# Layer 0 of an interleaved attention kernel: memory part added once per segment, two-chunk maps, filler matmuls

## Chip, cores, metric

One core of one Trainium2 chip. The metric is device time of one launch in microseconds (us), the span of the core. Ratios are the mean time of one kernel's fast runs over that of the other's of the same rounds, so not quite the ratio of the medians that I quote; brackets are 95% intervals.

## The reference, cut

Four layers over 2048 tokens of 512 features, 32 heads of 16: layers 0 and 2 are "A", layers 1 and 3 "B".

```python
def _A_ref(x, wq, wk, wv, wo, beta):             # 4 segments of 512 tokens
    ...
    for s in range(N):
        p = _softmax(qs @ ks * scale + mask)      # local attention, causal
        a_dot = p @ vs
        a_mem = (phi(qs) @ M) / (phi(qs) @ z + 1e-6)   # memory of earlier segments
        o = g * a_mem + (1.0 - g) * a_dot
        M = M + phi(ks).T @ vs ; z = z + sum(phi(ks))
    return concat(o) @ wo
def _B_ref(x, wqkv, wo): ...                      # full attention, 2048 x 2048
x = x + A(ln(x)); x = x + B(ln(x)); x = x + A(ln(x)); x = x + B(ln(x))
```

phi(t) is t+1 for positive t, else exp(t). So a segment of an A layer has a local part (softmax attention) and a memory part, which needs everything that earlier segments put into M and z.

## The kernel before: the parts concerned

The kernel is a program builder. It walks through the work with its own clock of each engine, decides at each moment what goes next, and emits fixed instruction streams. Attention units go first. Background threads (layer norm, projections, memory chain, output projection) get the PE when attention doesn't want it. ScalarE does the exponentials in groups of up to three 512-column tiles. Some quadruples of four tiles ("dz", "dx") get their exponential on VectorE instead. A table changes the builder's parameters every 110 groups, and strings give the order of A and B units:

```python
PAT = ["AAAAAAAA", "ABABABABBBABAAABBA", ...]
TUNE = [
    (0, {'CF': 0.829, 'PB': 0.02, 'DX_AHEAD': 0.5, 'DX_SLACK': 4.776, 'DX_LEAD': 69, ...}),
    (110, {'CF': 0.849, 'RATE': 0.472, 'MMC': 0.229}),
    ...                      # CF, PB, MMC, PV0: what the builder believes matmuls cost
```

`ensure(x)` makes the builder run background threads until x exists, and nothing else: each time the step that can start first, with 0.4 us added per place down the list of priorities. The end of a layer-0 chunk:

```python
if self.cnt[key] == 2:
    if A and s >= 2:
        self.ensure(("op", L, s - 2))        # buffer o0[s % 2] still feeds the projection of s-2
    ...
        o = dv(lambda e: e.transpose(dst, onf), ..., "oT", 0.73)
        if s > 0:
            self.ensure(("nd", L, s))        # memory part of this segment
            o = dv(lambda e: e.tensor_tensor(dst, dst, mem, ALU.add), ..., "oM", 0.43)
    self.chunk_done(L, s, c, zs, o)
```

and the test in front of a chunk's last value matmuls:

```python
if last and u["kind"] == "A" and u["s"] > 0 and (u["L"] > 0 or u["pvd"] == 4) and ("nd", u["L"], u["s"]) not in self.ev:
    return None
```

The memory part itself: eight steps of two products, reciprocal and multiply, then four transposing DMAs.

```python
for i in range(4):
    for hf in range(2):
        ...  # 2 matmuls ph x Mr ; den, reciprocal, multiply on DVE -> ot[i]
if L == 0:
    yield ("ev", [("pvdone", L, s - 1)])
    for i in range(4):
        self.dma_T(self.m0[:, :, i * 128:(i + 1) * 128], self.ot[:, i, :], ...)
self.set_ev(("nd", L, s), sc.t["dve"])
```

The maps phi work on chunks of 512 columns (exp on ACT; min, then max-and-add on DVE), 24 chunks of q and 24 of k. Filler matmuls exist (`keep_warm`), but are off (KEEP = 0).

The softmax here doesn't subtract the row's maximum and nothing guards it: scores larger than these inputs give would overflow.

## Time and profile before

| | before |
|---|---|
| median | 2082.59 us (2079.41 to 2085.5, 3 runs) |
| span of the profiled run | 2082.3 us |
| ACT busy / idle | 1990.4 / 91.9 us |
| mean granted TensorE clock | 0.649 |
| quadruples on VectorE | 109 |

A row of the profile's groups has line, engine, operation, output<-input, count, busy time and mean ns of one, then idle time before it and what ended it. In a timeline row a bracket is the engine's idle time just before, with its releaser. ACT is busy 96% of the time, so time is read from ACT's gaps and from what occupies it. The prediction shows the lines.

### The profile page before, as it was taken

What the parts mean: (1) busy time and instruction counts of PE and PEld (TensorE: products, weight loads), DVE (VectorE), ACT (ScalarE), POOL (GpSimd) and SP (SyncE); (2) the same over time, 40 slices, a digit from 0 to 9 for tenths busy, and PEclk for the clock granted to TensorE, in tenths of its full rate; (3) what the DMA queues carried; (4) which work ended last, traced back from release to release, by engine and by line L of the source; (5) the groups of instructions that cost most, each with busy time, mean ns of one, the idle gap of its engine ahead of it and who ended that gap; (6) DMA issues with size and microseconds to landing.
All of it is one profiled execution on the core that took longest, in us unless ns stands there. A gap on an engine that the chain in (4) does not pass through costs nothing.

```text
span 2082.3 us, 41423 instructions
## 1 busy us (share of the span) xinstructions
PE 1705.9 (82%) x17296; PEld 592.2 (28%) x17382; DVE 1645.9 (79%) x2492; ACT 1990.4 (96%) x1615; POOL 253.3 (12%) x564
## 2 busy tenths in 40 slices
PE   6768888888878888788787788888888888888887
PEld 2222221112311121212222223213444444444443
DVE  6886758887678688787878577688789988898986
ACT  6879899999999999999999999999999999999997
POOL 4542410001400000211013103100000000000000
PEclk9679897557565675557776797675655555555555
DMA  4210100001000000001010100100000000000000
GB/s 122 51 32 11 28 15 1 1 1 21 7 16 1 11 11 1 1 1 21 1 21 1 21 11 2 21 1 2 14 5 4 4 14 4 5 4 15 6 4 12
DMA packets 75467, 27.31 MB, mean 13 GB/s; under 512 B 68112, under 2 KB 74768, under 8 KB 75280
## 3 DMA queue, kind: packets, MB, share of 16 engines
q1 hardware_dynamic: 74176, 23.62, 5.2%
q8 instruction: 136, 2.23, 0.5%
q10 hardware_dynamic: 1104, 1.05, 0.2%
q14 instruction: 51, 0.42, 0.1%
HBM read 6.30 MB, written 2.10 MB: 4 GB/s over the span
## 4 chain that ended last, share of the span: by engine, by line
ACT 49%; PE 29%; issue 11%; DVE 7%; POOL 2%; DMA 1%; SPq 0%; ACTq 0%; DVEq 0%; POOLq 0%
ACT pT L1135 48%; PE ps L1128 13%; PE ps L625 6%; PE ps L1379 5%; PE ps L1397 4%; POOL pT L1158 2%; PE ps L1267 1%; DMA xT<-xn 1%; DVE lnst L662 1%; DVE T L1517 0%; DVE tokk L786 0%; ACT ph L780 0%; DVE ot L919 0%; SPq L444 0%; DVE db L1325 0%
## 5 line engine op out<-in xcount | busy, mean ns | idle before, releaser
L1135 ACT ACTIVATE pT<-ps 128x1536 bf16<-128x1536 f32 (+2 forms) x1525 | 1957.3, 1458 | 66.1 <-PE ps L1128 57.4
L1128 PE MATMUL ps<-q,kB 32*128 32x512 bf16 x3660 | 699.6, 546 | 256.3 <-ACT pT L1135 248.3
L1270 DVE TENSOR_SCALAR dz<-ps 128x512 int32<-128x512 f32 x436 | 301.0, 691 | 156.8 <-PE ps L1267 143.6
L1128 PEld LDWEIGHTS ps<-q,kB 32*128 32x128 bf16 x3660 | 131.4, 97 | 701.5 <-ACT pT L1135 656.1
L1158 POOL TENSOR_SCALAR_AFFINE_SELECT pT<-pT 128x256 bf16<-128x256 bf16 (+2 forms) x516 | 223.8, 463 | 613.4 <-ACT pT L1135 611.9
L1397 PE MATMUL ps<-pT,vB 128*17 128x512 bf16 x2216 | 278.7, 507 | 0.7 <-DVE q L640 0.5
L1267 PE MATMUL ps<-q,kB 32*128 32x512 bf16 x436 | 250.0, 573 | 0.0
L1379 PEld LDWEIGHTS ps<-vB,pT 128*128 128x128 bf16 x5776 | 181.1, 104 | 160.8 <-issue 157.6
L1379 PE MATMUL ps<-vB,pT 128*128 128x17 bf16 x5776 | 213.4, 177 | 0.7 <-ACT pT L1135 0.4
L1128 PE MATMUL ps<-q,kA 32*128 32x512 bf16 (+3 forms) x1024 | 122.4, 385 | 47.7 <-ACT pT L1135 45.6
L1307 DVE TENSOR_SCALAR df<-dz 128x2048 f16<-128x2048 uint16 x109 | 134.0, 1229 | 2.4
L1397 PEld LDWEIGHTS ps<-pT,vB 128*17 128x17 bf16 x2216 | 51.0, 89 | 187.0 <-issue 176.5
L1314 DVE TENSOR_SCALAR db<-dz 128x2048 int16<-128x2048 int16 x80 | 97.8, 1222 | 1.6 <-PE ps L1397 1.6
L1517 DVE STREAM_TRANSPOSE T<-ps 128x512 f32<-128x512 f32 x94 | 66.6, 709 | 15.3 <-PE ps L1397 14.7
L625 PE MATMUL ps<-xT,wB 128*128 128x512 bf16 x228 | 70.4, 429 | 7.4 <-issue 3.9
L625 PE MATMUL ps<-xT,wA 128*128 128x512 bf16 x238 | 68.7, 412 | 8.1 <-issue 2.1
L991 DVE TENSOR_TENSOR x_tok<-x_tok,ps 128x512 bf16<-128x512 bf16 x60 | 41.0, 686 | 41.6 <-PE ps L625 41.3
L1319 DVE TENSOR_TENSOR tokk<-tokk,df 128x2048 f16<-128x2048 f16 x58 | 70.7, 1219 | 0.7
L1323 DVE TENSOR_TENSOR tokk<-tokk,df 128x2048 f16<-128x2048 f16 x58 | 70.7, 1218 | 0.6
L1128 PEld LDWEIGHTS ps<-q,kA 32*128 32x128 bf16 x1024 | 29.9, 99 | 125.7 <-ACT pT L1135 110.9
L680 DVE TENSOR_SCALAR xn<-x_tok,lnmv,lnr 128x512 bf16<-128x512 bf16 x60 | 24.5, 429 | 50.3 <-DMA xT<-xn 49.4
L1325 DVE TENSOR_TENSOR db<-db,dz 128x2048 int16<-128x2048 int16 x51 | 62.8, 1231 | 1.2
(128 smaller groups left out, 1513.2 us busy)
## 6 DMA issues: line engine op xcount, KB each, us to landing
x_tok<-in_A_x_dram SPq DMA_DIRECT2D x14, 128.0 KB, 2.7
wB<-in_B_wqkv_dram SPq DMA_DIRECT2D x4, 384.0 KB, 3.9
out_dram<-x_tok SPq DMA_DIRECT2D x3, 512.0 KB, 3.0
xT<-xn SPq DMA_TRANSPOSE x60, 2.4
wA<-in_A_wk_dram SPq DMA_DIRECT2D x1, 512.0 KB, 7.7
wA<-in_A_wq_dram ACTq DMA_DIRECT2D x1, 512.0 KB, 7.9
wA<-in_A_wv_dram SPq DMA_DIRECT2D x1, 512.0 KB, 8.8
woA<-in_A_wo_dram SPq DMA_DIRECT2D x1, 512.0 KB, 7.5
```

The costliest lines, as they stand in the source:

```text
L625: return self.sc.add("pe", lambda e: e.matmul(out, lhsT, rhs, start=start, stop=stop), reads=reads, bank_ops=[(bank, "w", alloc)], emit=la ...
L1128: sc.add("pe", (lambda out, lhsT, rhs: lambda e: e.matmul(out, lhsT, rhs, start=True, stop=True))(out, lhsT, rhs), reads=reads, bank_ops=[ ...
L1135: o = sc.add("act", lambda e: e.activation(dst, src, ACT.Exp, scale=float(SCALE)), writes=[self.b_pT[s0 + i] for i in range(n)], bank_ops= ...
L1158: om = sc.add("pool", (lambda ap, pat: lambda e: e.affine_select(ap, ap, pattern=pat, compare_op=ALU.is_ge, fill=0.0, base=0, channel_mult ...
L1267: sc.add("pe", lambda e: e.matmul(out, lhsT, rhs, start=True, stop=True), reads=reads, bank_ops=[(bank, "w", alloc)], emit=True, name="SX" ...
L1270: o = sc.add("dve", lambda e: e.tensor_scalar(dst, out, float(EXP_C * 65536.0), -126.0 * 65536.0, op0=ALU.mult, op1=ALU.max), writes=[self ...
L1307: o = dv(lambda e: e.tensor_scalar(F, lo, 2.0 ** -16, -0.5, op0=ALU.mult, op1=ALU.add), bz, bF, "dF", 1.24)
L1314: o = dv(lambda e: e.tensor_scalar(E, hi, 128.0, 16256.0 + 53.0, op0=ALU.mult, op1=ALU.add), bz, bE, "dE", 1.24)
L1319: o = dv(lambda e: e.tensor_tensor(Pz, Pz, F, ALU.mult), bF + bP, bP, "dP2", 1.24)
L1323: o = dv(lambda e: e.tensor_tensor(Pz, Pz, F, ALU.mult), bF + bP, bP, "dP4", 1.24)
L1379: op = sc.add("pe", (lambda o0, w, v, first: lambda e: e.matmul(self.ps[:, o0:o0 + 17], w, v, start=first, stop=True, skip_group_check=Tru ...
L1397: sc.add("pe", (lambda out, v, rhs, start, stop: lambda e: e.matmul(out, v, rhs, start=start, stop=stop, skip_group_check=True))(out, v, r ...
```

## The change

Intent: the memory part should no longer hold up each chunk of layer 0. It is added to a whole segment later, by a background thread. Two chunks go through phi at once. And where PE would idle, matmuls with zero weights are meant to keep its clock high. Table and unit order were tuned anew. The core of the diff, cut:

```diff
-PAT = ["AAAAAAAA", "ABABABABBBABAAABBA", "BAAABBBAAAAA", "AAAAABABABAB", "AAAABABABBAA", "BBABAABAAA"]
+PAT = ["AAAAAAAA", "ABABABABBAABAABBBA", "AAAAABABBBAA", "AAAAABBABBAA", "AAAAABBBBAAA", "BBABAABAAA"]
-    (110, {'CF': 0.849, 'RATE': 0.472, 'MMC': 0.229}),
+    (110, {'DVE_AHEAD': 4.069, 'KEEP': 8.79}),
 ...                                             # all other rows too
+        if HALF and L % 2 == 0 and s > 0:       # q: mask, phi, mask on two chunks
+            cs = slice(2 * h, 2 * h + 2)
+            ...
+            yield from self.g_phi(L, s, qo, bo, self.ph[:, cs, :], self.b_ph[cs], f"q{c}", wide=True)
-            for c in range(NCH):                # k: phi on two chunks
+            for h in range(2):
 ...
             if self.cnt[k3] == 4:
+                self.set_ev(("pvl", L, s))
+                if L == 0 and s > 0:
+                    self.t_addmem(s, zs)
+                    return
+    def t_addmem(self, s, zs):
+            yield ("ev", [("nd", 0, s)])
+            ...
+            o = sc.add("dve", lambda e: e.tensor_tensor(dst, dst, mem, ALU.add), ..., name="oM", cost=1.24)
+            self.t_out(0, s, zs, self.prio_of(1, s) - 0.5, o.t_end)
-                if s > 0:
-                    self.ensure(("nd", L, s))
-                    o = dv(... "oM", 0.43)
-  ... and (u["L"] > 0 or u["pvd"] == 4) and ("nd", ...
+  ... and u["L"] > 0 and ("nd", ...
-            if KEEP and self.acc_open and t + d <= tc + KEEP_D and ... and self.pvu[0]["L"] <= KEEP_L:
+            if KEEP and t + d <= tc + KEEP_D and (...) <= sc.lately() < KEEP and self.keep_warm():
```

More of the change, by code (lines that the diff above doesn't have):

```diff
@@ L54 @@
 DX3 = 1
+HALF = True
 TUNE = [
-    (0, {'CF': 0.829, 'PB': 0.02, 'DX_AHEAD': 0.5, 'DX_SLACK': 4.776, 'DX_LEAD': 69, 'DVE_AHEAD': 4.525, 'MAXPV': 3, 'RATE': 0.606, 'MMC': 0.22, 'LN_G': 3, 'PV0': 0.371, 'DX3': 1}),
-    (110, {'CF': 0.849, 'RATE': 0.472, 'MMC': 0.229}),
-    (220, {'MMC': 0.213, 'PV0': 0.365}),
-    (330, {'LN_G': 2}),
-    (440, {'DVE_AHEAD': 2.5}),
-    (660, {'PB': 0.022}),
-    (880, {'PB': 0.026, 'RATE': 0.4}),
-    (990, {'MMC': 0.2, 'PV0': 0.324}),
-    (1100, {'CF': 1, 'PB': 0.025, 'DX_AHEAD': 0.676, 'LN_G': 3}),
-    (1210, {'PB': 0.036, 'DX_LEAD': 64, 'DVE_AHEAD': 3.61}),
-    (1320, {'DX_SLACK': 5.687}),
-    (1430, {'PB': 0.035, 'DX_LEAD': 53, 'DVE_AHEAD': 3.961, 'MAXPV': 2}),
+    (0, {'CF': 0.684, 'PB': 0.026, 'DX_AHEAD': 0.696, 'DX_SLACK': 4.776, 'DX_LEAD': 67, 'DVE_AHEAD': 4.525, 'MAXPV': 3, 'RATE': 0.606, 'MMC': 0.22, 'LN_G': 1, 'PV0': 0.371, 'DX3': 1, 'KEEP': 0.0, 'KEEP0': 3.0, 'KEEP_D': 0.0}),
+    (110, {'DVE_AHEAD': 4.069, 'KEEP': 8.79}),
+    (220, {'KEEP0': 4.5}),
+    (550, {'DX_SLACK': 6.455}),
+    (660, {'CF': 1}),
+    (770, {'MMC': 0.219, 'KEEP_D': 0.029}),
+    (880, {'PB': 0.037, 'DX3': 0}),
+    (990, {'DX_AHEAD': 0.893, 'MMC': 0.227, 'PV0': 0.34}),
+    (1100, {'PB': 0.038}),
+    (1210, {'MMC': 0.247}),
+    (1320, {'DX_SLACK': 8}),
+    (1430, {'CF': 0.748}),
 ]
@@ L320, in alloc @@
         self.ph = sb("ph", [P, NCH, 512], bf)
-        self.et = sb("et", [P, 512], bf)
+        self.et = sb("et", [P, 1024], bf)
         self.tokk = sb("tokk", [P, 4, D], bf)
@@ L346, in alloc @@
         self.gm = sb("gm", [P, NCH, 136], bf)
-        self.bmf = sb("bmf", [P, 136], f32)
+        self.bmf = self.et[:, 0:272].bitcast(f32)
         self.parm = sb("parm", [P, 2], f32)
@@ L397, in alloc @@
         self.b_gm = B("gm")
-        self.b_bmf = B("bmf")
+        self.b_bmf = self.b_et
         self.b_parm = B("parm")
@@ L769, in g_q @@
             return
+        if HALF and L % 2 == 0 and s > 0:
+            h = c // 2
+            key = ("cnt_q", L, s, h)
+            self.cnt[key] = self.cnt.get(key, 0) + 1
+            if self.cnt[key] < 2:
+                return
+            cs = slice(2 * h, 2 * h + 2)
+            qo, qe = self.q[:, z, 1, cs, :], self.q[:, z, 0, cs, :]
+            bo, be = self.b_q[z][1][cs], self.b_q[z][0][cs]
+            o = sc.add("dve", lambda e: e.tensor_scalar(qe, qo, self.parm[:, 0:1], None, op0=ALU.mult),
+                       reads=bo + [self.b_parm], writes=be, name=f"qm{L}{s}0", cost=0.45)
+            yield from self.g_phi(L, s, qo, bo, self.ph[:, cs, :], self.b_ph[cs], f"q{c}", wide=True)
+            o = sc.add("dve", lambda e: e.tensor_scalar(qo, qo, self.parm[:, 1:2], None, op0=ALU.mult),
+                       reads=bo + [self.b_parm], writes=bo, name=f"qm{L}{s}1", cost=0.45)
+            for x in (2 * h, 2 * h + 1):
+                self.set_ev(("q", L, s, x), o.t_end)
+            return
         sc.add("dve", lambda e: e.tensor_scalar(qe, qo, self.parm[:, 0:1], None, op0=ALU.mult),
@@ L776, in g_q, with g_phi @@
         self.set_ev(("q", L, s, c), o.t_end)
-    def g_phi(self, L, s, src, bsrc, dst, bdst, nm, res=None, bres=None):
+    def g_phi(self, L, s, src, bsrc, dst, bdst, nm, res=None, bres=None, wide=False):
         sc = self.sc
-        o = sc.add("act", lambda e: e.activation(dst, src, ACT.Exp), reads=[bsrc], writes=[bdst], name=f"phe{L}{s}{nm}", cost=0.65)
+        bsrc, bdst = ([x] if isinstance(x, Buf) else list(x) for x in (bsrc, bdst))
+        o = sc.add("act", lambda e: e.activation(dst, src, ACT.Exp), reads=bsrc, writes=bdst, name=f"phe{L}{s}{nm}", cost=1.07 if wide else 0.65)
         yield ("t", o.t_end, 0.0)
-        o = sc.add("dve", lambda e: e.tensor_scalar(dst, dst, 1.0, None, op0=ALU.min), reads=[bdst], writes=[bdst],
-                   name=f"phm{L}{s}{nm}", cost=0.29)
+        o = sc.add("dve", lambda e: e.tensor_scalar(dst, dst, 1.0, None, op0=ALU.min), reads=bdst, writes=bdst,
+                   name=f"phm{L}{s}{nm}", cost=0.43 if wide else 0.29)
         if res is None:
             res, bres = dst, bdst
-        o = sc.add("dve", lambda e: e.scalar_tensor_tensor(res, src, 0.0, dst, op0=ALU.max, op1=ALU.add), reads=[bsrc, bdst],
-                   writes=[bres], name=f"phs{L}{s}{nm}", cost=0.71)
+        o = sc.add("dve", lambda e: e.scalar_tensor_tensor(res, src, 0.0, dst, op0=ALU.max, op1=ALU.add), reads=bsrc + bdst,
+                   writes=bres if isinstance(bres, list) else [bres], name=f"phs{L}{s}{nm}", cost=1.24 if wide else 0.71)
         return o
@@ L822, in g @@
             if s >= 2:
-                w += [("pvdone", L, s - 2), ("dM", L, s - 2)]
+                w += [("pvdone" if L else "pvl", L, s - 2), ("dM", L, s - 2)]
             yield ("ev", w)
@@ L862, in g @@
             self.set_ev(("phk", L, s))
-            for c in range(NCH):
+            for h in range(2):
                 yield ("t", o.t_end, 0.0)
-                tk = self.tokk[:, :, c * 128:(c + 1) * 128]
-                et = self.et[:, :].rearrange("p (i f) -> p i f", i=4)
-                o = yield from self.g_phi(L, s, tk, self.b_tokk[c], et, self.b_et, f"k{c}", tk, self.b_tokk[c])
+                tk = self.tokk[:, 2 * h:2 * h + 2, :].rearrange("p i f -> p (i f)")
+                o = yield from self.g_phi(L, s, tk, self.b_tokk, self.et[:, :], self.b_et, f"k{h}", tk, self.b_tokk, wide=True)
             for c in range(NCH):
@@ L1485, in chunk_done @@
         if self.cnt[k3] == 4:
+            self.set_ev(("pvl", L, s))
+            if L == 0 and s > 0:
+                self.t_addmem(s, zs)
+                return
             self.set_ev(("otfree", L, s))
@@ L1488, in chunk_done, with g @@
             self.t_out(L, s, zs, self.prio_of(L + 1, s) - 0.5, o.t_end)
+    def t_addmem(self, s, zs):
+        sc = self.sc
+        def g():
+            yield ("ev", [("nd", 0, s)])
+            yield ("t", max(self.sc.t["pe"], max(b.last_write.t_end for b in self.b_m0)), 0.0)
+            dst, mem = (x.rearrange("p c t -> p (c t)") for x in (self.o0[s % 2], self.m0))
+            bd = list(dict.fromkeys(self.b_o0[s % 2]))
+            o = sc.add("dve", lambda e: e.tensor_tensor(dst, dst, mem, ALU.add), reads=bd + self.b_m0, writes=bd, name="oM", cost=1.24)
+            self.set_ev(("otfree", 0, s))
+            self.set_ev(("pvdone", 0, s))
+            self.t_out(0, s, zs, self.prio_of(1, s) - 0.5, o.t_end)
+        self.spawn(g(), self.prio_of(1, s) - 0.6, f"OM{s}")
     def users(self, bufs):
@@ L1549, in norm @@
             if A:
-                dst, mem, bd = self.o0[s % 2][:, c, :], self.m0[:, c, :], self.b_o0[s % 2][c]
+                dst, bd = self.o0[s % 2][:, c, :], self.b_o0[s % 2][c]
                 o = dv(lambda e: e.transpose(dst, onf), [self.b_on], [bd], "oT", 0.73)
-                if s > 0:
-                    self.ensure(("nd", L, s))
-                    o = dv(lambda e: e.tensor_tensor(dst, dst, mem, ALU.add), [bd] + self.b_m0, [bd], "oM", 0.43)
             else:
@@ L1745, in pv_ready @@
         first, last = self.pv_ends(u)
-        if last and u["kind"] == "A" and u["s"] > 0 and (u["L"] > 0 or u["pvd"] == 4) and ("nd", u["L"], u["s"]) not in self.ev:
+        if last and u["kind"] == "A" and u["s"] > 0 and u["L"] > 0 and ("nd", u["L"], u["s"]) not in self.ev:
             return None
@@ L1846, in run @@
             tc = min([x for x in (rs, rp, rx) if x is not None], default=to)
-            if KEEP and self.acc_open and t + d <= tc + KEEP_D and (0.0 if sc.warm else KEEP0) <= sc.lately() < KEEP and self.pvu and self.pvu[0]["L"] <= KEEP_L:
-                self.keep_warm()
+            if KEEP and t + d <= tc + KEEP_D and (0.0 if sc.warm else KEEP0) <= sc.lately() < KEEP and self.keep_warm():
                 continue
@@ L1857, in keep_warm @@
     def keep_warm(self):
-        bank = self.acc_bank
-        self.sc.add("pe", lambda e: e.matmul(self.ps[:, bank.col0:bank.col0 + 512], self.zw[:, :], self.wA[:, 0, 0:512], start=False, stop=False,
-                                             skip_group_check=True),
-                    reads=[self.b_zw, self.b_wA[0]], bank_ops=[(bank, "w", self.acc_alloc)], emit=False, name="D", cost=0.215, cold=0.2133, work=1.0)
+        sc = self.sc
+        if self.acc_open:
+            bank, alloc, start = self.acc_bank, self.acc_alloc, False
+        else:
+            bank = self.free_bank()
+            if bank.t_free + 0.12 > sc.t["pe"]:
+                return False
+            alloc, start = self.new_alloc(), True
+        sc.add("pe", lambda e: e.matmul(self.ps[:, bank.col0:bank.col0 + 512], self.zw[:, :], self.wA[:, 0, 0:512], start=start, stop=start,
+                                        skip_group_check=True),
+               reads=[self.b_zw, self.b_wA[0]], bank_ops=[(bank, "w", alloc)], emit=False, name="D", cost=0.215, cold=0.2133, work=1.0)
+        return True
     def ensure_any(self):
```

## The prediction

> **What bounds the kernel now.** I began with the page: first the busy shares, then the forty slices.
>
> ```profile
> span 2082.3 us, 41423 instructions
> PE 1705.9 (82%) x17296; PEld 592.2 (28%) x17382; DVE 1645.9 (79%) x2492; ACT 1990.4 (96%) x1615; POOL 253.3 (12%) x564
> ...
> ACT  6879899999999999999999999999999999999997
> ...
> PEclk9679897557565675557776797675655555555555
> ```
>
> ScalarE (ACT) is the bound: 1990.4 of 2082.3 us. All that a change can win is its 91.9 us of idle time plus whatever work it takes off that engine. The idle tenths are at the left, in layer 0, and in the last slice. The granted TensorE clock is near one half over most of the span.
>
> Second, busy time per stretch (columns: length, then PE, PEld, DVE, ACT, POOL busy us with counts, clock, DMA share, GB/s), to see where the 91.9 us lie.
>
> ```profile
> 0.00:30.00 30.00, 17.31 (x109) 6.65 (x110) 16.85 (x36) 13.62 (x17) 14.17 (x35) 1.00 0.39 117
> 30.00:60.00 30.00, 24.74 (x215) 8.51 (x211) 26.14 (x61) 28.76 (x35) 14.80 (x36) 0.97 0.41 95
> 60.00:120.00 60.00, 48.84 (x404) 15.50 (x406) 50.05 (x117) 52.48 (x55) 34.43 (x81) 0.70 0.26 53
> 120.00:180.00 60.00, 39.55 (x339) 12.59 (x345) 47.95 (x113) 43.66 (x46) 28.77 (x67) 0.77 0.14 28
> 180.00:300.00 120.00, 103.11 (x765) 30.94 (x775) 78.34 (x165) 114.06 (x108) 29.04 (x73) 0.93 0.07 14
> 300.00:420.00 120.00, 96.90 (x618) 21.00 (x621) 101.08 (x140) 117.96 (x100) 0.00 (x0) 0.66 0.03 5
> 420.00:1440.00 1020.00, 831.76 (x6779) 234.88 (x6819) 778.41 (x1210) 996.53 (x796) 132.11 (x272) 0.66 0.04 9
> 1440.00:2070.00 630.00, 535.68 (x8056) 258.98 (x8068) 543.60 (x648) 621.56 (x465) 0.00 (x0) 0.52 0.03 7
> ```
>
> Length minus ACT busy gives idle time: 16.4 us in the start-up, 1.2, then 7.5 and 16.3 in the two stretches where layer 0 carries the memory (60 to 180), 5.9, 2.0, 23.5 over the long middle, 8.4 in layer 3; the rest, some 10 us, is the tail after 2070.
>
> Third, the timeline around the worst hole, and what the waits say of it.
>
> ```profile
> 138.20 1.46 ACT L1135 ACTIVATE pT<-ps 128x1536 bf16<-128x1536 f32 x1
> 143.71 0.63 ACT L780 ACTIVATE et<-tokk 128x512 bf16<-128x512 bf16 x1 [4.05 <-DVE sm L914]
> 150.54 1.03 ACT L1135 ACTIVATE pT<-ps 128x1024 bf16<-128x1024 f32 x1 [6.20 <-PE ps L1128]
> ...
> ACT pT L1135 <- PE ps L1128: 57.4, 62, 6.6
> ```
>
> Between 139.7 and 150.5 ACT does 0.63 us of work. In that time the trace shows the eight division steps of the memory part on DVE, one after another, each with a PE step between, and the four transposing DMAs into the upper half of dz. No score matmul is issued. This is the forced wait in the layer-0 epilogue: a finished chunk needs the memory part ("nd") before it may add it, so the program builder runs all remaining memory work there and then, in program order, while attention stands. A smaller copy of it is at 75 to 91, with 2.41 and 2.52 us of ACT idle.
>
> Fourth, the ACT and DVE groups by form, for unit costs.
>
> ```profile
> L1135 ACT ACTIVATE pT<-ps 128x1536 bf16<-128x1536 f32 x1254 | 1731.7, 1540 | 44.4 <-PE ps L1128 38.1 <-PE ps L1267 2.3 <-POOL pT L1158 1.3
> L1135 ACT ACTIVATE pT<-ps 128x1024 bf16<-128x1024 f32 x267 | 287.5, 1083 | 15.1 <-PE ps L1128 12.7 <-POOL pT L1158 1.8 <-PE ps L1267 0.4
> L780 ACT ACTIVATE et<-tokk 128x512 bf16<-128x512 bf16 x24 | 17.7, 736 | 4.0 <-DVE sm L914 4.0
> L780 ACT ACTIVATE ph<-q 128x512 bf16<-128x512 bf16 x24 | 16.6, 690 | 0.1
> L1270 DVE TENSOR_SCALAR dz<-ps 128x512 int32<-128x512 f32 x436 | 301.0, 691 | 156.8 <-PE ps L1267 143.6 <-PE ps L1128 2.9 <-PE ps L1379 1.2
> ```
>
> The last line is the second lever: 436 score tiles, 109 quadruples of four, get their exponential on DVE instead of ACT.
>
> **What the Trainium skill says.** "TensorE: Matmul & The Clock Gate", section "What's actually happening": the PE clock is half rate by default and becomes full after about 3.4 us of sustained work. The trace agrees: 15-us stretches read 0.50 in pure attention and 1.00 where projections run. "ScalarE: Activation LUTs", section "What ACT_TABLE_LOAD costs": an ACTIVATE with immediate scale and bias takes 186 ns plus 0.833 ns per column, so one wide instruction saves a fixed part. The trace is close: from 1083 and 1540 ns above, 0.89 ns per column and a fixed 169 ns. "VectorE: DVE Perf Modes", section "The perf-mode tier table (the rule you actually need)": a 2048-wide bf16 tensor_tensor takes 1224 ns, a tensor_scalar 693. The trace has 1219 to 1231 and 682 to 698.
>
> **The change part by part.**
>
> *Memory part added once.* Removed: twelve adds of 512 columns (8 at 469 ns, 4 at 459; 5.6 us) and the wait before them, also at the test that held back a chunk's last value matmuls. Added: three adds of 2048, 1.22 us each, 3.7 us, once per segment, which wait as a background thread. So 1.9 us off DVE, little by itself. What counts is the hole: out of 23.8 us idle between 60 and 180 I credit 16. Eight stay, since the same stretches also wait on masks (POOL) and on projections, and since value storage, output projection and the next layer norm still come after the memory part. Of the 7.1 us in 30 to 60 and 180 to 300 I credit 2.
>
> *Two-chunk maps on ACT.* 48 exponentials of 512 columns cost 34.3 us. They become 24 of 1024. One costs 713 ns on average plus 512 columns at 0.89, about 1.17 us: 28.1 us. Saved: 6.2 us, all on the bound.
>
> *Two-chunk maps on DVE.* Minimum: 48 at 315 ns become 24 at about 440 (between 315 and the 690 of 2048 columns), 4.5 us less. Max-and-add: 48 at 707 become 24 at about 1.22 us, 4.6 less. Parity masks: 48 at 365 become 24 at about 494 (2048 take 751), 5.7 less. With the adds, 16.7 us off DVE, which isn't the bound.
>
> *More tiles on DVE.* A quadruple costs DVE four evictions at 0.691 plus 1.23+1.22+0.69+1.22+0.69+1.22+1.22, so 10.25 us, and takes 4 x 1540/3 = 2.05 us off ACT. DVE relief gives up to 1.6 quadruples. The new order puts the last memory chunks of layer 0 earlier by about one unit, and the DVE path opens only once layer 0 is out (first at 311 us; 109 in 1760 us is one per 16 us): one more. Looser tuning of how far DVE may run ahead: one or two more. I take four, 8 us.
>
> *Filler matmuls.* They keep the clock high where PE is idle. ACT waits for scores only 57.4 us in all and some 29 us after 300 us, so a warm PE can give little: out of 23.5 us in the middle I credit 6, together with the new tuning and order. Fillers add PE work but no ACT work; a filler that begins just before a real score delays it by 0.2 us (warm) to 0.4 (cold), and coarser pairs delay the first scores of a segment: I charge 2 us.
>
> Sum: 16 + 2 + 6.2 + 8 + 6 - 2 = 36 us. 2082.6 - 36 gives about 2046 us, 1.7% less.
>
> **The rivals.**
>
> *The wait only moves.* Output projection and layer norm of a segment still need the memory part, and later layer-1 chunks need those. Then ACT would starve somewhat later, in the stretch from 180 to 300, and only the wide maps and a few quadruples remain: about 2068. For it: the memory chain itself (transposes, maps, products, eight divisions) is no shorter. Against: layer-1 work of earlier segments is there to fill in, and ACT idles only 5.9 us there now.
>
> *The warm clock does more than I think.* DVE waits 143.6 us for the scores of its own tiles, and PE is busy 82% at a clock of 0.65. If fast matmuls let DVE take its tiles sooner, ten to twelve more quadruples would take another 12 to 16 us off ACT, to about 2030. Against: those scores go out beside ACT's groups, every 1.5 us, and their pace is ACT's, not PE's.
>
> *The fillers hurt.* If the builder's clock model is wrong they sit in front of real scores. ACT at 99% in layers 1 and 3 has no slack, so 0.05 us on each of 1500 groups would cost up to 75 us, and the time would be back at 2080 or above. Against: they are placed only where the next ready work is further away than a filler is long, and this tuning was presumably chosen by measurement.
>
> **Range and chances.** The firm part (wide maps, most of the hole) is 20 to 25 us; quadruples and middle are the uncertain 14, from 0 to 30. So 2022 to 2070 should hold it 8 times in 10. Two per cent is 41.7 us, a line at 2041, just below my value: 0.40 for faster, 0.57 within, 0.03 slower.
>
> **What would show it.** Right: no ACT gap over 5 us between 60 and 180; ACT idle there under 10 us; 24 exponentials of 1024 columns near 1.17 us; ACT busy lower by 12 to 16 us; 432 to 460 evictions into dz; a mean clock well above 0.65 from the filler matmuls with no more ACT waits for scores. Wrong: the hole at another place, a higher ACT wait for PE, or a count of quadruples that moves by more than eight. The answer then lies in the tuning, not in the named parts.

## More of the kernel before

```profile
145.34 0.41 PE L625 MATMUL ps<-Mr,ph 128*128 128x136 bf16 x2 [0.42 <-DVE ot L919]
145.67 0.60 PE L1397 MATMUL ps<-pT,vA 128*17 128x384 bf16 x8
147.16 0.63 PE L625 MATMUL ps<-vA,tokk 128*128 128x136 bf16 x4 [0.89 <-DVE ot L919]
148.39 1.49 PE L625 MATMUL ps<-woA,dz 128*128 128x512 bf16 x3 [0.60 <-DVE ot L919]
149.81 0.61 PE L1128 MATMUL ps<-q,kA 32*128 32x512 bf16 x2
```

The products of the eighth and last division step (Mr,ph) start at 145.34. The chunk's last value matmuls (pT,vA), which the test above holds until the memory part exists, follow them at 145.67. Then come matmuls for the update of M and an output projection (woA) that reads dz, the home of o0[0]: segment 0's projection, the last that `ensure(("op", 0, 0))` waits for. Scores go out again at 149.81. So two waits stand in a row: the test until 145.7, then the projection.

## The result, and the profile after

After: 2071.32 us median (2069.83 to 2072.68, 4 runs), before 2081.0 in the same rounds: ratio 0.995 [0.9931, 0.997]. So 10 us faster, within 2%, and just outside the predicted range of 2022 to 2070. The page after:

```profile
span 2070.5 us, 42307 instructions
PE 1759.0 (85%) x17826; PEld 622.1 (30%) x17826; DVE 1632.5 (79%) x2425; ACT 1983.8 (96%) x1584; POOL 264.2 (13%) x568
...
ACT  6959999999999999999999999999999999999998
...
PEclk9779899569557995589955999596555555555555
```

The span fell by 11.8 us: ACT has 6.6 us less work (1990.4 to 1983.8) and 5.2 us less idle time (91.9 to 86.7). The idle digit at the third slice went from 7 to 5: layer 0 got worse. The stretches say the same:

```profile
60.00:120.00 60.00, 50.74 (x412) 15.44 (x414) 45.91 (x99) 52.71 (x52) 36.15 (x82) 0.75 0.28 54
120.00:180.00 60.00, 43.36 (x341) 14.96 (x342) 45.35 (x101) 40.96 (x40) 30.63 (x69) 0.80 0.14 27
180.00:300.00 120.00, 108.79 (x793) 32.17 (x791) 83.11 (x169) 114.75 (x108) 29.92 (x74) 0.93 0.09 18
300.00:420.00 120.00, 101.84 (x677) 22.90 (x676) 101.97 (x136) 119.71 (x99) 0.00 (x0) 0.75 0.00 1
420.00:1440.00 1020.00, 874.09 (x7331) 262.48 (x7327) 782.98 (x1190) 1002.84 (x791) 136.22 (x273) 0.77 0.05 9
```

ACT idle from 60 to 180 is 7.3 + 19.0 = 26.3 us, where it was 23.8. From 420 to 1440 it is 17.2 (was 23.5), and the clock there rose from 0.66 to 0.77. The timeline around the gap, ACT and then PE:

```profile
134.63 1.02 ACT L1153 ACTIVATE pT<-ps 128x1024 bf16<-128x1024 f32 x1
...
153.31 2.36 ACT L1153 ACTIVATE pT<-ps 128x1536 bf16<-128x1536 f32 x2 [17.66 <-PE ps L1146]
...
148.37 4.46 PE L626 MATMUL ps<-woA,dz 128*128 128x512 bf16 x12 [0.42 <-DVE ot L937]
152.76 0.60 PE L1146 MATMUL ps<-q,kA 32*128 32x256 bf16 x9
```

There is now one gap of 17.7 us. It ends in the same way as before: segment 0's output projection, this time with twelve of its sixteen matmuls still to do. The gap holds all eight division steps and the update of M. Nine score matmuls follow the projection at once (152.76), before ACT copies out anything newly projected (155.56): attention still had work, the builder had not let it go out. And the groups of the maps, tiles on VectorE and fillers:

```profile
L799 ACT ACTIVATE et<-tokk 128x1024 bf16<-128x1024 bf16 x12 | 13.8, 1152 | 0.1
L799 ACT ACTIVATE ph<-q 128x1024 bf16<-128x1024 bf16 x12 | 13.5, 1128 | 1.0 <-DVE q L641 1.0
...
L1288 DVE TENSOR_SCALAR dz<-ps 128x512 int32<-128x512 f32 x440 | 302.9, 689 | 150.5 <-PE ps L1285 140.3 <-PE ps L1397 4.1 <-DVE db L1332 0.2
...
L1900 PE MATMUL ps<-wA,zw 128*128 128x512 bf16 x444 | 133.0, 385 | 0.0
```

440 evictions are 110 quadruples, one more, and not four. There are 444 fillers.

### The profile page after: what moved, and what is told of

Its sections match the earlier page's. It is cut to its first block, busy times and chain, and to the rows that moved or that the text cites. A ratio compares the mean times of both kernels' runs of the same rounds, so it can differ in the third digit from the quotient of the medians.

```text
span 2070.5 us, 42307 instructions
## 1 busy us (share of the span) xinstructions
PE 1759.0 (85%) x17826; PEld 622.1 (30%) x17826; DVE 1632.5 (79%) x2425; ACT 1983.8 (96%) x1584; POOL 264.2 (13%) x568
## 4 chain that ended last, share of the span: by engine, by line
ACT 33%; PE 15%; issue 6%; DVE 1%; POOL 1%; DMA 0%; SPq 0%; ACTq 0%; DVEq 0%; POOLq 0%
ACT pT L1153 33%; PE ps L1146 7%; PE ps L1397 3%; PE ps L626 3%; PE ps L1415 1%; POOL pT L1176 1%; PE ps L1285 1%; PE ps L1900 0%; DMA xT<-xn 0%; ACT ph L799 0%; DVE lnst L663 0%; DVE dz L1341 0%; DVE df L1325 0%; DVE dz L1288 0%; ACT et L799 0%
## 5 line engine op out<-in xcount | busy, mean ns | idle before, releaser
L1146 PE MATMUL ps<-q,kB 32*128 32x512 bf16 x3656 | 655.8, 513 | 218.9 <-ACT pT L1153 202.8
L1288 DVE TENSOR_SCALAR dz<-ps 128x512 int32<-128x512 f32 x440 | 302.9, 689 | 150.5 <-PE ps L1285 140.3
L1176 POOL TENSOR_SCALAR_AFFINE_SELECT pT<-pT 128x256 bf16<-128x256 bf16 (+2 forms) x520 | 233.5, 481 | 568.2 <-ACT pT L1153 566.6
L1415 PE MATMUL ps<-pT,vB 128*17 128x512 bf16 x2216 | 251.6, 456 | 3.3 <-DVE T L1554 1.1
L1285 PE MATMUL ps<-q,kB 32*128 32x512 bf16 x440 | 240.6, 547 | 0.3 <-DVE dz L1288 0.3
L1146 PE MATMUL ps<-q,kA 32*128 32x256 bf16 (+3 forms) x1024 | 125.8, 390 | 47.4 <-ACT pT L1153 45.1
L1325 DVE TENSOR_SCALAR df<-dz 128x2048 f16<-128x2048 uint16 x110 | 135.7, 1233 | 1.6
L1900 PE MATMUL ps<-wA,zw 128*128 128x512 bf16 x444 | 133.0, 385 | 0.0
L626 PE MATMUL ps<-xT,wB 128*128 128x512 bf16 x256 | 78.1, 435 | 0.0
L671 POOL TENSOR_SCALAR lnr<-lnmv 128x4 f32<-128x4 f32 x15 | 5.5, 369 | 510.8 <-DVE lnmv L666 510.8
L1341 DVE TENSOR_TENSOR tokk<-tokk,df 128x2048 f16<-128x2048 f16 x56 | 68.2, 1218 | 0.7
L1337 DVE TENSOR_TENSOR tokk<-tokk,df 128x2048 f16<-128x2048 f16 x56 | 68.2, 1218 | 0.5
L1341 DVE TENSOR_TENSOR dz<-dz,df 128x2048 f16<-128x2048 f16 x54 | 66.5, 1232 | 1.3
```

The source lines that it names most:

```text
L626: return self.sc.add("pe", lambda e: e.matmul(out, lhsT, rhs, start=start, stop=stop), reads=reads, bank_ops=[(bank, "w", alloc)], emit=la ...
L1146: sc.add("pe", (lambda out, lhsT, rhs: lambda e: e.matmul(out, lhsT, rhs, start=True, stop=True))(out, lhsT, rhs), reads=reads, bank_ops=[ ...
L1176: om = sc.add("pool", (lambda ap, pat: lambda e: e.affine_select(ap, ap, pattern=pat, compare_op=ALU.is_ge, fill=0.0, base=0, channel_mult ...
L1285: sc.add("pe", lambda e: e.matmul(out, lhsT, rhs, start=True, stop=True), reads=reads, bank_ops=[(bank, "w", alloc)], emit=True, name="SX" ...
L1288: o = sc.add("dve", lambda e: e.tensor_scalar(dst, out, float(EXP_C * 65536.0), -126.0 * 65536.0, op0=ALU.mult, op1=ALU.max), writes=[self ...
L1325: o = dv(lambda e: e.tensor_scalar(F, lo, 2.0 ** -16, -0.5, op0=ALU.mult, op1=ALU.add), bz, bF, "dF", 1.24)
```

## The experiments

Theory 1: the hole in layer 0 is as long as the memory chain; taking one wait away lets it start at another. Rival: the wait for segment 0's projection, now reached earlier, is the whole cause. Theory 2: the gain came from the new table, or from the fillers' clock, and not from the memory part.

### Single parts on the old table: mem_alone, wide_alone

```diff
 # mem_alone: the kernel before, plus only
+ t_addmem, "pvl", pv_ready without the layer-0 case;  - ensure(("nd", L, s)) and the per-chunk "oM"
 # wide_alone: the kernel before, plus only
+ HALF = True, g_phi(..., wide=True) for q and k, et 1024 columns wide
```

> The kernel before with the memory part added in one step and nothing else changed (old tables, narrow maps, no fillers). Theory 1, the hole only moves: ScalarE's idle time from 60 to 180 us stays at 20 to 30 us (before 23.8), and since every later group falls elsewhere than the old tables were tuned for, the total gets worse, by 10 to 50 us. Rival, the prediction's: idle time from 60 to 180 falls to about 8 us and the total to about 2066 us.

> The kernel before with the two-chunk maps and nothing else changed. The prediction's sizes: ScalarE busy time falls by 6.2 us for the same count of exponential tiles. Rival: back-to-back ACTIVATEs overlap, so a narrow one costs less than its duration and the saving is about 2 us. The total says little here: with tables tuned for another order it may be 10 to 30 us longer, and if it isn't, the tables matter less than I now think.

mem_alone 2124.48 us, ratio 1.0204 [1.0187, 1.022]; wide_alone 2102.03 us, 1.0093 [1.0077, 1.011]. The stretches of mem_alone:

```profile
60.00:120.00 60.00, 49.92 (x437) 15.51 (x438) 50.54 (x117) 55.91 (x56) 38.55 (x90) 0.71 0.26 52
120.00:180.00 60.00, 38.19 (x316) 13.86 (x323) 46.48 (x111) 39.20 (x42) 24.74 (x59) 0.80 0.15 30
```

ACT idle 4.1 + 20.8 = 24.9 us from 60 to 180, before 23.8: the small copy of the hole at 75 to 91 shrank, the big one grew. So the memory part doesn't shorten the hole, with none of the other parts there. The rest of the 43 us comes later (900 to 1440 lost 32 us more of ACT time than before: 489.35 busy of 540, before 521.26), where the code is unchanged and only the table no longer fits. That makes totals of single parts on the old table no measure of the parts.

For the maps I compared starts of back-to-back ACT instructions over the whole trace: from a narrow map exponential to the next start the median is 0.520 us (44 cases before), from a wide one 0.947 us (23 after, 23 in wide_alone). Two rows each from the timelines of before and after show it:

```profile
121.35 0.66 ACT L780 ACTIVATE et<-tokk 128x512 bf16<-128x512 bf16 x1
...
121.87 1.48 ACT L1135 ACTIVATE pT<-ps 128x1536 bf16<-128x1536 f32 x1
```

```profile
121.38 1.06 ACT L799 ACTIVATE et<-tokk 128x1024 bf16<-128x1024 bf16 x1
122.34 1.01 ACT L1153 ACTIVATE pT<-ps 128x1024 bf16<-128x1024 f32 x1
```

The narrow one lasts 0.66 us but the next begins after 0.52; the wide one 1.06 and 0.96. A pair saves 2 x 0.520 - 0.947 = 0.093 us, 24 pairs 2.2 us. The 6.2 us of the prediction counted durations, which overlap.

### Where the hole goes: own_buffer, no_division

```diff
 # own_buffer: the changed kernel; segment 2 writes to db, idle until layer 0 is out
+        self.o0 += [self.db[:, :, :], self.o0[1]]
+        self.b_o0 += [[self.b_db] * 4, self.b_o0[1]]
 ...                                    # o0[s] for o0[s % 2] wherever it is used
-            if A and s >= 2:
+            if A and s >= 3:
                 self.ensure(("op", L, s - 2))
 # no_division: the changed kernel (wrong on purpose)
-                for hf in range(2):
+                for hf in range(2 if L or s != 2 else 0):
```

> The changed kernel, but segment 2 of layer 0 writes its output to the buffer db (idle until layer 0 is out) instead of the one that segment 0's output projection still reads, so nothing is forced when its first chunk ends. Theory 1, the hole only moves: ScalarE's long gap (17.7 us from 135.7) starts some 7 us later, ends about as late as before, and the total stays within 3 us of the changed kernel's. Rival, this forced projection is the whole cause: the gap goes, and the total falls by about 15 us.

own_buffer 2074.65 us, ratio to before 0.9971 [0.9957, 0.9986]; the changed kernel had 0.995. Its timeline of ACT:

```profile
137.08 4.65 ACT L1155 ACTIVATE pT<-ps 128x1536 bf16<-128x1536 f32 x4 [0.82 <-POOL pT L1178]
154.79 0.60 ACT L641 ACTIVATE kA<-ps 128x512 bf16<-128x512 f32 x1 [13.06 <-PE ps L628]
```

With the buffer conflict gone, ACT goes on until 141.7 instead of 135.7, then stops for 13.1 us. Idle from 120 to 180 is 19.4 us, as good as the 19.0 with the conflict. Exponentials come back only at 161.0; until then ACT runs four copies. The total came out 3.3 us above the changed kernel's median, just outside the 3 us expected. The rival's 15 us did not appear: the projection was only the place where the builder stood.

> The changed kernel, but the eight steps of segment 2's memory read (two products, reciprocal and multiply each) are left out; its result is wrong on purpose. Theory 1, the long gap at 135 us is the length of the memory chain itself, with attention work used up: ScalarE idle from 120 to 180 us falls from 19.0 to 10 us or less and no gap over 5 us is left there. If the gap comes from waiting for the forced projection alone: idle stays at 15 us or more. The total means little, since later groups fall elsewhere than tuned for.

no_division 2076.09 us (2 runs; the eight steps are left out on purpose, though the run's check of the result still passed). Its stretch:

```profile
120.00:180.00 60.00, 48.59 (x388) 15.44 (x389) 45.09 (x87) 53.34 (x53) 31.19 (x68) 0.86 0.14 28
```

Idle falls from 19.0 to 6.7 us, and the longest ACT wait from 60 to 180 is 3.8 us. So the divisions of segment 2's memory read, eight steps in which DVE and PE take turns (in the changed kernel 0.8 to 1.9 us from one to the next, once 3.9), make up most of the hole. Both together bear out theory 1: taking one wait away moves the hole, taking the chain's own work away shrinks it. They don't show that attention has to stand that long. A builder that puts segment 0's projection, or the value matmuls, in front of the chain was not tried. What exactly stops attention in own_buffer meanwhile (room in the ring of exponentials, a PSUM bank that background work takes) I saw in the builder's plan only; no run separates them.

### Fillers: no_filler, tiny_filler

```diff
 # no_filler: the changed kernel
-    (110, {'DVE_AHEAD': 4.069, 'KEEP': 8.79}),
+    (110, {'DVE_AHEAD': 4.069, 'KEEP': 0.0}),
 # tiny_filler: the changed kernel, same place, one column
-  e.matmul(self.ps[:, bank.col0:bank.col0 + 512], self.zw[:, :], self.wA[:, 0, 0:512], ...)
+  e.matmul(self.ps[:, bank.col0:bank.col0 + 1], self.zw[:, :], self.wA[:, 0, 0:1], ...)
```

> The changed kernel with the filler matmuls switched off and its tables kept. Prediction's size: fillers are worth a few us at most, so at most 2080 us. Rival, the tables were tuned with the fillers in place and no longer fit: 2100 to 2130 us, with the additional ScalarE idle time after 900 us, where nothing of layer 0 is left. The granted clock falls from 0.71 to about 0.65.

> The changed kernel with every instruction in its place on every engine, but each of the 444 filler matmuls streams 1 column instead of 512, so it keeps no clock high. If the fillers' worth is the clock: granted clock about 0.65 instead of 0.71, ScalarE waits for scores grow, and the time is 2085 to 2110 us, most of the way to the kernel without fillers (2109 us). If their worth is only that the table was tuned around them (the order of the other instructions): 2066 to 2075 us, as the changed kernel.

no_filler 2108.98 us, 1.013 [1.0115, 1.0146], clock 0.643. tiny_filler 2089.69 us, 1.004 [1.0023, 1.0057], clock 0.637. Against before of the same rounds the changed kernel stands at 0.995, so at equal order the wide fillers are worth 0.9% or some 18 us; the other 19 us to no_filler are order. ACT's longest waits from 900 to 1440, after and then no_filler:

```profile
ACT pT L1153 <- PE ps L1146: 6.7, 12, 1.1
```

```profile
ACT pT L1153 <- PE ps L1146: 33.8, 32, 8.6
```

And the same scores in the changed kernel, then in tiny_filler, there with the fillers themselves:

```profile
L1146 PE MATMUL ps<-q,kB 32*128 32x512 bf16 x3656 | 655.8, 513 | 218.9 <-ACT pT L1153 202.8
```

```profile
L1146 PE MATMUL ps<-q,kB 32*128 32x512 bf16 x3656 | 703.5, 550 | 229.4 <-ACT pT L1153 218.6
...
L1900 PE MATMUL ps<-wA,zw 128*128 128x1 bf16 x444 | 44.8, 173 | 0.0
```

Same instructions in the same places, slower matmuls, 18 us. The fillers' worth in this kernel is the clock, and it is three times what I credited.

### A first search of the tables, and why it failed

I searched TUNE and PAT anew for four codes, by random steps of one or two entries, for about as long each, keeping what the builder's own clock called faster. Diff: only these tables, 15 rows of the form shown further below.

> The kernel before, code unchanged, with only its tuning table and unit order searched again for as long as the other three of this call. Theory 2, most of the measured 10 us came with the new table and not with the three named parts: this one gains as much, 2062 to 2074 us. Rival, the parts give the gain and the old table was already as good as it can be: 2078 us or more.

> The memory part in one step, alone, with the table searched again. The prediction: 15 us or more faster than the retuned kernel before. Theory 1, the hole only moves: not faster than the retuned kernel before, rather up to 8 us slower; ScalarE idle from 60 to 180 us at 20 us or more.

> The two-chunk maps alone, with the table searched again. The prediction's sizes: 6 us from ScalarE plus up to 3 from VectorE, so 9 us faster than the retuned kernel before. Sized by start-to-start times (0.52 us narrow, 0.95 wide): 2.2 us plus what VectorE gives, so 2 to 5 us faster.

> The changed kernel, code unchanged, table searched again for as long. If the retuning is worth the same to any version, some 10 to 18 us faster than the changed kernel: 2052 to 2062 us, with the gain after 900 us and the gap at 135 us untouched. If the changed kernel's table was already at its best: 2068 us or more.

| code | us | ratio to before |
|---|---|---|
| before_retuned (no part) | 2076.77 | 0.997 [0.9955, 0.9985] |
| mem_retuned | 2080.95 | 0.9994 [0.9977, 1.0011] |
| wide_retuned | 2089.38 | 1.0028 [1.0013, 1.0043] |
| after_retuned (all parts) | 2073.21 | 0.9948 [0.9932, 0.9965] |

A new table alone gave 0.3% at best, less than the change; all parts gained nothing over the changed kernel. My expectation of a gain from a table alone was wrong in size. mem_retuned is 4 us slower than before_retuned, with 23.9 us of ACT idle from 60 to 180, as theory 1 said. wide_retuned is a miss: 13 us slower, where both sizes said faster. The search had a flaw: the table also holds CF, PB, MMC and PV0, the costs with which the builder judges itself. It could look faster by believing in cheaper matmuls.

### A second search, judged by fixed costs

Again by the builder's clock, but timed by three fixed sets of matmul costs. "fitted" and "second" are two seeds. All start from the changed kernel's table except none_fitted and filler_only, which start from the table before.

> First of four versions whose tables were searched for the same time, this time judged by three fixed sets of matmul costs (in the earlier search the table also held the costs that judged it, which is why those gains didn't come out). This one has none of the three parts: the kernel before with a better table. If the parts carry the gain: 2074 to 2082 us. If a new table alone does: 2071 us or less.

> The changed kernel without fillers, table fitted to that. If the fillers' clock is worth what the one-column fillers suggest (18 us), it is 10 to 20 us slower than the fitted kernel with all parts. Prediction's size: at most 6 us slower.

> Wide maps and fillers, but the memory part is added chunk by chunk as before, with its wait; table fitted to that. Prediction: 15 us or more slower than the fitted kernel with all parts, with the gap of before at 140 us. Theory 1, the hole only moves: within 4 us of the one with all parts, either way.

> The changed kernel with its table searched again in the same way, the one to compare the other three with. 2060 to 2072 us; if it is not faster than the changed kernel, the fitted tables are no better than the one that came with the change, and differences under some 8 us between such versions are chance of the table.

> As no_mem_fitted, its table searched anew from another seed. If adding chunk by chunk is really better, 2060 to 2068 us and faster than all_second; if the 8 us of the first pair were chance of the table, as slow as all_second or slower (the plan gives this table 3 us less good a time than all_second).

> As all_fitted, from the other seed: 2064 to 2075 us. Its distance from all_fitted (2070.6) says how much is chance of the table.

> Memory part in one step and fillers, but maps chunk by chunk as before, table fitted to that. From the start-to-start times the wide maps give 2.2 us on ScalarE and up to 3 us by way of VectorE: 3 to 8 us slower than all_second. The prediction's sizes: 6 plus 3 us slower.

> The kernel before with the filler matmuls alone, table fitted to that. If the fillers carry the gain of the change: 2065 to 2073 us, as fast as the changed kernel. If they need the other parts: 2078 us or more.

| kernel | memory once | wide maps | fillers | us | ratio to before |
|---|---|---|---|---|---|
| none_fitted | no | no | no | 2084.15 | 1.0017 [1.0, 1.0033] |
| no_filler_fitted | yes | yes | no | 2088.28 | 1.0035 [1.002, 1.005] |
| all_fitted | yes | yes | yes | 2070.64 | 0.9952 [0.9938, 0.9967] |
| all_second | yes | yes | yes | 2071.62 | 0.9938 [0.9922, 0.9955] |
| no_mem_fitted | no | yes | yes | 2062.78 | 0.991 [0.9896, 0.9925] |
| no_mem_second | no | yes | yes | 2072.91 | 0.9948 [0.9925, 0.9971] |
| no_wide_second | yes | no | yes | 2071.71 | 0.9938 [0.9923, 0.9953] |
| filler_only | no | no | yes | 2075.09 | 0.9952 [0.9937, 0.9968] |

Read it by columns. Of the kernels with a table of their own, in both searches, those with fillers lie at 2063 to 2075 us (ratios 0.991 to 0.995), those without at 2077 (before_retuned) to 2089 (0.997 to 1.0035). Fillers alone, on the code before, give 0.48%, what the whole change gives. A lucky table without any part gave 0.3% (before_retuned), and the two intervals overlap; so that it is the fillers rests on tiny_filler too, where nothing else differed. Without the memory part the two seeds give 2062.8 and 2072.9, with it 2070.6 and 2071.6: the 8 us of the first pair did not come back, so I don't call the memory part harmful, only without a gain that shows. Its predicted 15 us are excluded by both pairs. Leaving out the wide maps changed nothing (0.9938 both); 2 us wouldn't show beside a spread of 10 us between two tables of the same code (no_mem).

As to what I expected: none_fitted is slower than both of its ranges, filler_only falls between its two, no_wide_second isn't slower than all_second at all, and no_mem_fitted is 8 us faster than all_fitted where theory 1 allowed 4; the second seed took that back. The other four came out as one of their cases said.

The hole stayed under every table. In the 19 kernels with the whole calculation ACT idles 21.1 to 28.5 us from 60 to 180: 21.5 to 26.9 in the 11 that add the memory once, 21.1 to 28.5 in the 8 that add it chunk by chunk.

filler_only shows how little else is needed. Its page:

```profile
PE 1773.0 (86%) x18105; PEld 645.9 (31%) x18273; DVE 1642.1 (79%) x2490; ACT 1989.4 (96%) x1615; POOL 254.0 (12%) x568
```

ACT's work is that of before (1990.4), the gain is in idle time, and the mean clock was 0.760.

no_mem_fitted beats both kernels, by 0.9% against before. Its code is that of the changed kernel without the memory part, with this order and these first rows of 15:

```diff
+PAT = ["AAAAAAAA", "AAABABBBBABBAABAAB", "AAAAABABBBAA", "AAAAABBABBAA", "AAAAABBBBAAA", "BABAABABAA"]
+    (0, {'CF': 0.684, 'PB': 0.037, 'DX_AHEAD': 0.713, 'DX_SLACK': 2.696, 'DX_LEAD': 64, 'DVE_AHEAD': 4.525, 'MAXPV': 3, 'RATE': 0.606, 'MMC': 0.22, 'LN_G': 1, 'PV0': 0.371, 'DX3': 1, 'KEEP': 0.0, 'KEEP0': 6.0, 'KEEP_D': 0.062}),
+    (110, {'DVE_AHEAD': 4.069, 'KEEP': 8.79, 'LN_G': 0, 'DX_SLACK': 3.869, 'KEEP0': 3.0, 'PB': 0.026, 'RATE': 0.618, 'MAXPV': 2, 'KEEP_D': 0.061, 'DX_LEAD': 68, 'PV0': 0.371}),
+    ...
```

It still has its hole in layer 0 (12.5 us at 147), so the hole stays the largest single thing to win there.

## Why the prediction was wrong, point by point

**Bound and stretches.** Right: ACT stayed the bound at 96%, and time followed its idle time plus its work.

**Readings.** Between 139.7 and 150.5 lie six of the eight division steps, not all; the first two are at 132.0 and 135.4. "The trace agrees", on the clock, holds for its two levels alone: the stretches of pure attention at 0.50 have PE busy for some 80%, see the last section. The TENSOR_SCALAR rows of 682 to 698 ns are f16; those that read or write 16-bit integers take 1220 to 1229, and the sum for a quadruple had this right.

**The hole, "I credit 16".** This is the step that failed. Measured: 2.5 us more idle from 60 to 180, so 18.5 us of the missing 24. I had put the hole down to "the forced wait in the layer-0 epilogue", for "nd", and let it end with that wait. By the code and the PE lines above, what held the scores back was first the test in front of the last value matmuls, which I had named in passing, and then a wait that the change keeps, for segment 0's projection. With the test gone the chunk ends earlier, and `ensure(("op", 0, 0))` runs what is left of the chain, and the projection, before any attention: a gap of 17.7 us. With that wait gone too (own_buffer) idle stays at 19.4 us from 120 to 180; without the eight steps (no_division) it is 6.7. What I credited to a wait belongs to the chain's work, which the builder lets run in front of attention. My own first rival, "the wait only moves", said that the chain is no shorter; I gave it too little. It named the wrong place, though: the wait reappeared at the same point, not from 180 to 300. Idle in 30 to 60 and 180 to 300, credited with 2 us less, went from 7.2 to 7.9. The rival's figure, 2068, is close to the measured 2071, but partly by luck: of its wide maps' 6.2 us 2.2 came and one quadruple of a few, and the fillers, which it left out, made up for them.

**Maps on ACT, 6.2 us.** Mechanism right, size wrong: 2.2 us, since back-to-back instructions overlap: a narrow map took 0.520 us from start to start, not its 0.713.

**Maps on DVE, 16.7 us off.** By the groups of the two profiles: minimum 15.2 to 10.6, max-and-add 33.9 to 29.6, masks 29.3 to 23.2, adds 5.5 to 3.6; together 16.9 less. Right. But it bought little:

**Four more quadruples, 8 us.** One came. A tile is worth 1331/3 ns of ACT (the median start-to-start time of a group of three), so a quadruple is 1.8 us, not 2.05. DVE still waited 140.3 us for its scores (before 143.6) at a higher clock. That fits my argument against the second rival, that the pace of ACT's groups rules, which I didn't apply to my own four; no run tests it.

**Middle, 6 us.** Right in size, 23.5 to 17.2 us, but by luck, since what does it was misjudged. I took the fillers for a small help, "a warm PE can give little"; tiny_filler shows 18 us for their clock, and filler_only, with a table fitted to it, the whole gain of the change. The 29 us of waits after 300 us in the kernel before left room for that; I credited a fifth of them.

**Fillers hurt, the third rival.** Not so.

**ACT work.** It fell by 6.6 us: 2.2 from maps, 1.8 from a quadruple, 1.4 from three evictions fewer (36 to 33, 0.48 us each start to start); 1.2 us I can't assign.

## What to carry to other kernels

Before crediting a removed wait, ask how long the work is that was waited for, and what the program would wait for next; here it stopped at the next buffer, with the same work in front of it. Price an instruction on a full engine by the time to the next start, not by its duration. In a kernel whose schedule is searched, a single part on the old table measures the misfit of the table: fit each version alike, with more than one seed, and judge by costs that the search can't change.

## What the Trainium skill lacked or had wrong

- "TensorE: Matmul & The Clock Gate", section "Why this matters for your kernels", advises to keep TensorE busy for over 4 us to reach the full clock. Busy time alone isn't enough: the stretch below of the kernel before has PE busy 81.8 of 100 us, with scores that use 32 rows, at a clock of 0.50. PE's longest gap there is 0.74 us and its longest unbroken run 4.8 us. Whether the gaps or the 32 rows do it, no run separates.

```profile
600.00:700.00 100.00, 81.77 (x497) 14.51 (x493) 76.79 (x92) 99.31 (x77) 0.00 (x0) 0.50 0.02 3
```

- The same page, section "Seeing it yourself", says that all-zero operands don't trip the peak-current limit, but no page says whether they count as activity for the clock. Matmuls with all-zero weights (the moving operand isn't zero) do: in the same places, 444 of them with 512 columns gave a mean clock of 0.709, with 1 column 0.637.
- "ScalarE: Activation LUTs", section "What ACT_TABLE_LOAD costs", was right for the maps: its 186 ns, less its 93 ns of overlap, plus 0.833 ns per column are 520 and 946 ns, and the traces have 520 and 947 from start to start. I had quoted the 186 ns without the overlap. For ACTIVATEs that read ps (PSUM, all of them f32) the fixed part is smaller: 478, 905 and 1331 ns from start to start for 512, 1024 and 1536 columns, so 51 ns and 0.833 per column; the page gives one overlap for all. It lacks that durations in a full stream are no measure: means of groups of 1536 columns rose from 1540 to 1574 ns with the change, while the median from start to start stayed at 1331.
